# When ScalarE copies what VectorE transposed, and where a weight conversion is spread, in a retention + squared-ReLU kernel

## The chip, the core and the metric

The kernel runs on one core of a Trainium2 chip. Time is the device time of one execution in microseconds (us). The engines are called by the names that the profile uses: PE is TensorE's matmul and PEld its weight load, DVE is VectorE, ACT is ScalarE, POOL is GpSimd, and SP issues the transfers (DMA). Each engine runs its own list of instructions from first to last; engines wait for each other by semaphores.

## What is computed

Two layers, both in fp32. The first is retention: for each of 8 batches and 8 heads, 576 positions of 64 values, scores of queries and keys are multiplied by a lower triangular matrix of decays and then by the values. The second is a feed-forward block with a squared ReLU on the 4608 x 512 result.

```python
scores = scale * np.matmul(q, k.transpose(0, 1, 3, 2))            # (8, 8, 576, 576)
Dmat = np.where(rel >= 0, gamma[:, None, None] ** rel[None, :, :], 0.0)
attn = np.matmul(scores * Dmat[None], v)                          # (8, 8, 576, 64)
x = attn.transpose(0, 2, 1, 3).reshape(4608, 512)
h = np.maximum(x @ w_in, 0.0)                                     # w_in  512 x 2048
out = (h * h @ w_out).astype(np.float32)                          # w_out 2048 x 512
```

The weights arrive as 64-bit floats; the kernel converts them to fp32 itself, with integer and float operations on DVE and ACT. Both large products are done with a seven-product scheme (four quadrants of each operand, sums of quadrants, seven products in place of eight).

## The kernel before

There are two phases. In the first, retention and the first product `x @ w_in` run interleaved, and the squared result goes to memory (`g_dram`). The second phase is the product with `w_out`. Retention goes in 40 chunks of 128 or 64 positions (five to a batch). The first product goes in nine blocks of 512 tokens. Block 0 uses plain matmuls; blocks 1 to 8 have 28 steps each (four passes of seven products, 8 matmul records a step), run by `ffn_in(n, mp, j)` with `j` from 0 to 6.

Three PSUM tiles, called a, b and c, take the seven products in the order a b c a b c b. A product that adds to a tile cannot begin until DVE has read what the tile held at the product before it: the seventh product (b) waits for the read after the fifth (b, line 635), and only the sixth stands between.

```python
        if j == 0:
            nc.scalar.copy(p1, p)                                            # line 626, ACT
        elif j == 1:
            nc.vector.tensor_tensor(u2, p, p1, op=ALU.add)                   # 628
        elif j == 2:
            nc.vector.tensor_tensor(p15, p, p1, op=ALU.add)                  # 630
        elif j == 3:
            nc.scalar.activation(g["A11"], p, AF.Relu)                       # 632
            nc.gpsimd.tensor_tensor(g["A11"], g["A11"], g["A11"], op=ALU.mult)   # 633, POOL
        elif j == 4:
            nc.vector.tensor_tensor(g["A22"], p, p15, op=ALU.add)            # 635
            square(g["A22"])                                                 # 623
        elif j == 5:
            nc.vector.tensor_tensor(g["S3"], p, u2, op=ALU.add)              # 639
            square(g["S3"])
        else:
            nc.vector.tensor_tensor(g["A12"], p, p1, op=ALU.add)             # 642
            square(g["A12"])
            queue.extend(g_sums(n, mp))      # four sums of quadrants, lines 554 to 557, one a step
        # ... (sums of the next block's x, lines 540 to 543; sums of w_in during block 1, 245 to 248)
        if n >= 3 or n_w2[0] < 3 + 2 * 5:
            if not (held[0] and type(w_out_next[0]) is tuple):
                n_w2[0] += 1
                # ... takes one part of w_out's conversion from its list and issues it
```

The conversion of w_out is a list of 139 parts, 16 pieces of 128 x 512 and the sums of their quadrants. A piece has five: `one` (DVE, line 210), `two` (DVE, 214) together with `beside` (ACT, lines 218 and 219), `three` (DVE, 222, which reads what `beside` wrote), `four` (DVE, 225) and `last` (DVE, 228, and the next fetch). The sums are on lines 245 to 248. They use a staging area in weight tile 6. The x of the third block (block 2) lies in weight tile 6 too; the x of the others takes turns in two rooms:

```python
    xT = {n: xT_room[n % 2 if n < 2 else (n - 3) % 2] for n in range(N_BLK)}
    xT[2] = W[6][:, 0:N_DM * TOK].rearrange("p (c t) -> p c t", c=N_DM)
```

From chunk 9 on, q and k are turned by DVE (`flip`, two transposes of 32 x 32 squares a chunk, line 392), and ACT then puts the squares in place (16 copies of 32 x 256 for a chunk of 128, 8 for one of 64, line 403):

```python
    def spread(i):
        t, to = st[i]["flip"], new_qk(i)
        for b in range(chunks[i][3] // 32):
            for g in range(4):
                moves.append((i, to[32 * g:32 * g + 32, :, :, 32 * b:32 * b + 32], t[32 * b:32 * b + 32, g, :, :, :]))
    def move(count, i=N_CH):
        while moves and count and moves[0][0] <= i:
            nc.scalar.copy(*moves.pop(0)[1:])                                # line 403, ACT
            count -= 1
    # ... in the loop over chunks, past the first five:
            retain_a(i - 1)
            move(C, i)               # whatever copies of chunk i are left, all at once
            ffn(i - 1, 0)            # about half of the steps that fall to this chunk
            retain_b(i - 1)          # ends in a small ACT copy, line 495, that retain_c waits for
            scores(i)                # PE reads the copies of chunk i; DVE's mask follows, line 443
            retain_c(i - 1)
            if N_TURN <= i + 1 < N_CH:
                spread(i + 1)
            if N_TURN <= i + 2 < N_CH:
                flip(i + 2)          # both transposes here
            ffn(i - 1, 1)            # the other half of the steps
```

Inside `ffn`, each step is preceded by `move(3)`.

Of the kernel before, what the change touches and what calls it, by code (L numbers as in the profile page):

```python
# [9 lines left out]
F32 = mybir.dt.float32  # L10
# [5 lines left out]
C = 128  # L16
CH = C // 2
TOK = 512
# [22 lines left out]
def kernel(  # L41
# [33 lines left out]
    nc = tc.nc  # L75
# [268 lines left out]

    st = {i: {} for i in range(N_CH)}
    u_ps = [None]

    xT = {n: xT_room[n % 2 if n < 2 else (n - 3) % 2] for n in range(N_BLK)}
    xT[2] = W[6][:, 0:N_DM * TOK].rearrange("p (c t) -> p c t", c=N_DM)

# [30 lines left out]
    def new_qk(i):  # L383
        t = work3.tile([128, 2, HP, C], F32, tag="qk", name="qk")
        st[i]["qT"], st[i]["kT"] = t[:, 0, :, :], t[:, 1, :, :]
        return t

    def flip(i):
        cs = chunks[i][3]
        t = st[i]["flip"] = work2.tile([128, 4, 2, HP, 32], F32, tag="flip", name="flip")  # L390
        for j in (1, 0):
            nc.vector.transpose(t[:cs, :, j, :, :], loaded[i][j][:cs].rearrange("s (p e) (d a) -> s (e d) p a", e=2, d=2))

    def spread(i):
        t, to = st[i]["flip"], new_qk(i)
        for b in range(chunks[i][3] // 32):
            for g in range(4):
                moves.append((i, to[32 * g:32 * g + 32, :, :, 32 * b:32 * b + 32], t[32 * b:32 * b + 32, g, :, :, :]))

    def move(count, i=N_CH):  # L400

        while moves and count and moves[0][0] <= i:
            nc.scalar.copy(*moves.pop(0)[1:])  # L403
            count -= 1

    def turn(i):
# [90 lines left out]
    def retain_c(i):  # L497

        b_, ci, c0, cs = chunks[i]
        own, grow = within(i, 0)  # L500
        more = ci + 1 < NCH
        for j in range(0, len(own), 2):
            for f in own[j:j + 2] + (grow[j:j + 2] if more else []):
                f()
        tok = b_ * S + c0
        at = tok
        p = xp[0][:, :, 0:256].rearrange("p a (g t) -> p a g t", g=2)
        while at < tok + cs:
            n = at // TOK

            while steps and steps[0][0] <= (n - 2 if n > 4 else n - 3):
                step()
            end = min(tok + cs, (n + 1) * TOK)
            nc.scalar.copy(xT[n][:, :, at - n * TOK:end - n * TOK].rearrange("p (a g) t -> p a g t", a=2),
                           p[:, :, :, at - tok:end - tok])
            if more and at == tok:
                grown(i, 1)
            at = end
            if n_next[0] < N_BLK and (n_next[0] + 1) * TOK <= at:
                steps.extend(block_steps(n_next[0]))  # L520
                n_next[0] += 1
        st[i] = loaded[i] = None
# [78 lines left out]
    def ffn_in(n, mp, j):  # L601

        if j == 0 and mp == 0:

            if n not in sums_x:
                sums_x[n] = sum_x(n)
            for f in sums_x[n]:
                f()
        left, right, to = PRODUCTS[j]
        if j in OPENS:  # L610
            sums[to] = ps_f.tile([128, 2, HT], F32, tag="f", name=f"h_{to}")
        p = sums[to]
        for mm in range(2):
            w = w_in[mp][:, mm, WI_SLOT[left], :, :]
            for c in range(2):
                nc.tensor.matmul(p[:, mm, :], lhsT=w[:, c, :], rhs=xs[n][right][:, c, :],  # L616
                                 start=(j in OPENS and mm == 0 and c == 0), stop=(j in CLOSES and c == 1),
                                 skip_group_check=True)
        g = g_of(mp)
        p1, u2, p15 = (p_room[mp % 2][:, s, :, :] for s in range(3))  # L620

        def square(t):
            nc.vector.scalar_tensor_tensor(t, t, 0.0, t, op0=ALU.max, op1=ALU.mult)  # L623

        if j == 0:
            nc.scalar.copy(p1, p)  # L626
        elif j == 1:
            nc.vector.tensor_tensor(u2, p, p1, op=ALU.add)
        elif j == 2:
            nc.vector.tensor_tensor(p15, p, p1, op=ALU.add)  # L630
        elif j == 3:
            nc.scalar.activation(g["A11"], p, AF.Relu)  # L632
            nc.gpsimd.tensor_tensor(g["A11"], g["A11"], g["A11"], op=ALU.mult)  # L633
        elif j == 4:
            nc.vector.tensor_tensor(g["A22"], p, p15, op=ALU.add)  # L635
            square(g["A22"])
        elif j == 5:

            nc.vector.tensor_tensor(g["S3"], p, u2, op=ALU.add)
            square(g["S3"])  # L640
        else:
            nc.vector.tensor_tensor(g["A12"], p, p1, op=ALU.add)  # L642
            square(g["A12"])
            queue.extend(g_sums(n, mp))

        if mp == N_MP - 1 and j in (3, 4, 5) and n_next[0] > n + 1:
            if n + 1 not in sums_x:
                sums_x[n + 1] = sum_x(n + 1)
            sums_x[n + 1].pop(0)()
        if j in (6, 0, 1, 2, 3):  # L650
            some(2 if n == 1 and mp == 0 else 1)
        if n == 1 and 1 <= j < 5 and mp + 1 < N_MP:
            sums_w.setdefault(mp + 1, sum_w_in(mp + 1)).pop(0)()

        if n >= 3 or n_w2[0] < 3 + 2 * 5:
            if not (held[0] and type(w_out_next[0]) is tuple):
                n_w2[0] += 1
                f = w_out_next[0]
                w_out_next[0] = next(w_out_steps, None)
                for f in f if type(f) is tuple else (f,):  # L660
                    f and f()
            if n == N_BLK - 2 and (mp, j) in ((2, 3), (3, 3)):
                assert w_out_next[0] is None
                fetch_w2(mp - 2)
# [4 lines left out]
    w_out_steps = w_out_parts()  # L669
    w_out_next = [next(w_out_steps)]  # L670
    held = [False]
    n_w2 = [0]

    def block_steps(n):
# [23 lines left out]
    def ffn(i, half):  # L698

        gone[0] += chunks[max(0, min(i, N_CH - 1))][3] / 2  # L700
        if steps and steps[0][0] == 0:

            move(6)
            for f in (step, lambda: convert(6)) if half else (lambda: convert(6), step):
                f()
            if half and steps and steps[0][0] == 0:
                step()
                convert(6)
            return
        if not behind:  # L710
            behind.append((gone[0] - HALF, done[0]))
        points = behind + [p for p in PACE if p[0] > behind[0][0]]
        want = points[-1][1]
        for (x0, y0), (x1, y1) in zip(points, points[1:]):
            if gone[0] < x1:
                want = y0 + (y1 - y0) * (gone[0] - x0) / (x1 - x0)
                break
        count = max(1, int(want) - done[0])
        while steps and count:
            held[0] = half == 0 and count == 1  # L720
            move(3)
            step()
            count -= 1
        held[0] = False


    def warm(count, wide):
# [12 lines left out]
    for i in range(N_CH + 1):  # L740
        if i <= N_EARLY:

            if i == 1:
                convert(2)
            elif i == 2:
                convert(5)
            if i >= 1:
                retain_a(i - 1)
                if i < 3:
                    warm(4, False)  # L750
                else:
                    convert(1)
                    first_in(2 * i - 5, (0,))
                    convert(5)
                retain_b(i - 1)
                if i < 3:
                    warm(4, False)
                retain_c(i - 1)
            convert((0, 1, 1, 0, 1)[i])
            if i == N_EARLY:  # L760
                fetch_raw(2)
                step()
            scores(i)
            if i == 2:
                convert(5)
                first_in(0, (0,))
            elif i == 3:
                convert(1)
                first_in(2, (0,))
                convert(5)  # L770
            elif i == N_EARLY:
                convert(5)
                step()
                convert(6)
            scale_q(i + 1, nc.gpsimd)
            if i < N_EARLY:
                if i < 2:
                    warm(6, False)
                turn(i + 1)
        else:  # L780
            if i == N_EARLY + 1:
                gone[0] = TOK
            retain_a(i - 1)
            if i < N_TURN:
                turn(i)
            move(C, i)
            ffn(i - 1, 0)
            retain_b(i - 1)
            if i < N_CH:
                scores(i)  # L790
            retain_c(i - 1)
            if N_TURN <= i + 1 < N_CH:
                spread(i + 1)
            if N_TURN <= i + 2 < N_CH:
                flip(i + 2)
            ffn(i - 1, 1)
# [249 lines left out]
```

## Time and profile before

The median of three runs is 996.27 us (995.36 to 997.81). The profiled execution spans 994.4 us. Read by stretches:

| stretch, us | what runs | PE busy | DVE busy | ACT busy |
|---|---|---|---|---|
| 0 to 106 | first chunks, block 0, conversion of w_in | 94.33 | 75.99 | 48.52 |
| 106 to 562 | retention and blocks 1 to 8 interleaved | 437.81 | 396.51 | 265.24 |
| 562 to 994 | last steps, then the product with w_out | 428.37 | 316.17 | 36.39 |

Costs of one instruction that the change touches, from the groups of instructions (mean): copy on line 403, 402 ns, 440 of them; a transpose on line 392, 697 ns for k and 664 ns for q; lines 210, 214, 222, 225 and 228 of the conversion, 506, 472, 757, 814 and 756 ns; lines 218 and 219 on ACT, 722 and 670 ns; a sum on lines 245 to 248 some 520 to 660 ns as mean of its shapes; a PSUM read on lines 628 to 642, 681 to 687 ns.

The profile names engines, lines and tiles as in the code above. A wait is written "engine tile line <- releaser": how long the engine was idle in total before instructions of that line, how many times, and the longest single time. A row of the windows view gives a stretch of time, then each engine's busy time in it with the number of instructions, the clock granted to TensorE as a share of full speed, the share of DMA engines in use and the GB/s they moved.

### The profile page before, as it was taken

The page shows a single profiled execution, that of the slowest core. Times are in us where ns is not written, and L with a number is a line of the kernel's source. Part 1 is how long each engine was busy: PE and PEld are TensorE (multiplying, and loading weights), DVE is VectorE, ACT ScalarE, POOL GpSimd, SP SyncE. Part 2 cuts the span into 40 slices and gives each one's busy share as a digit, 9 for nine tenths or more (in the row PEclk, how much of TensorE's full clock was granted, in tenths as well). Part 3 has the DMA queues.
Part 4 walks back from the last instruction along what each step waited for, and adds up shares of the span by engine and source line. Part 5 has one row for each costly group of instructions (what it writes and reads, how often), then busy time and mean ns, then how long its engine had stood idle before and what let it go on. Part 6 is the DMA issues. An engine that isn't in the chain of part 4 may idle for free. (4 is left out here: it accounts for less than half of the span.)

```text
span 994.4 us, 24115 instructions
## 1 busy us (share of the span) xinstructions
PE 960.5 (97%) x10092; PEld 855.8 (86%) x10092; DVE 788.7 (79%) x1458; ACT 350.2 (35%) x871; POOL 131.9 (13%) x121
## 2 busy tenths in 40 slices
PE   7899999999999989989999999999999999999998
PEld 6655777888878778877788889999999999999998
DVE  4789798768889899998986777777777677777766
ACT  3445575765665756746651000000000000000000
POOL 3211222212223231312211000000000000000000
PEclk9999999999999999989999999999999999999999
DMA  8884657655697589769358999684673757556351
GB/s 199 245 239 114 184 171 207 191 146 181 204 303 231 172 251 257 218 185 301 109 200 303 402 401 336 233 280 174 234 263 141 274 191 269 192 218 215 125 212 44
DMA packets 185037, 219.19 MB, mean 220 GB/s; under 512 B 118624, under 2 KB 135008, under 8 KB 175968
## 3 DMA queue, kind: packets, MB, share of 16 engines
q1 hardware_dynamic: 182816, 217.13, 67.3%
q8 instruction: 79, 1.29, 0.5%
q10 hardware_dynamic: 2112, 0.52, 0.2%
q14 instruction: 30, 0.25, 0.1%
HBM read 128.23 MB, written 89.39 MB: 219 GB/s over the span
## 5 line engine op out<-in xcount | busy, mean ns | idle before, releaser
L616 PE MATMUL h_b<-room,w 128*128 128x256 f32 x736 | 181.9, 391 | 10.6 <-DVE room L635 4.3
L403 ACT COPY qk<-flip 32x256 f32<-32x256 f32 x440 | 177.0, 402 | 6.3
L616 PEld LDWEIGHTS h_b<-room,w 128*128 128x128 f32 x736 | 139.9, 193 | 33.2 <-DVE room L635 6.1
L903 PE MATMUL o_b<-w,room 128*128 128x128 f32 x1168 | 144.5, 275 | 0.7 <-DVE room L854 0.7
L903 PEld LDWEIGHTS o_b<-w,room 128*128 128x128 f32 x1168 | 137.2, 192 | 0.9 <-DVE room L854 0.9
L903 PE MATMUL o_c<-w,room 128*128 128x128 f32 x1008 | 123.0, 275 | 0.0
L903 PEld LDWEIGHTS o_c<-w,room 128*128 128x128 f32 x1008 | 117.7, 192 | 0.0
L616 PE MATMUL h_c<-room,w 128*128 128x256 f32 x480 | 115.9, 385 | 0.0
L917 ACT COPY r<-o_a 128x128 f32<-128x128 f32 x53 | 14.1, 266 | 272.5 <-PE o_a L903 241.9
L616 PE MATMUL h_a<-room,w 128*128 128x256 f32 x448 | 107.6, 383 | 0.0
L616 PEld LDWEIGHTS h_c<-room,w 128*128 128x128 f32 x480 | 91.9, 193 | 13.6 <-DVE room L642 0.3
L616 PEld LDWEIGHTS h_a<-room,w 128*128 128x128 f32 x448 | 83.7, 190 | 12.1 <-ACT room L626 0.3
L633 POOL TENSOR_TENSOR room<-room 128x512 f32<-128x512 f32 x32 | 36.9, 1152 | 370.4 <-ACT room L632 264.5
L903 PE MATMUL o_a<-w,a 128*128 128x128 f32 x688 | 85.6, 275 | 0.0
L903 PEld LDWEIGHTS o_a<-w,a 128*128 128x128 f32 x688 | 81.2, 192 | 0.1
L623 DVE SCALAR_TENSOR_TENSOR room<-room 128x512 f32<-128x512 f32 x96 | 72.3, 753 | 3.3
L580 PE MATMUL h_ps<-room,w 128*128 128x512 f32 (+1 forms) x160 | 58.7, 515 | 3.3 <-DVE w L228 2.5
L375 POOL TENSOR_TENSOR q_ld<-q_ld,dv 128x512 f32<-128x512 f32 (+1 forms) x39 | 48.6, 1245 | 76.7 <-DMA q_ld<-in_q_dram 50.6
L457 PEld LDWEIGHTS x_ps<-qk,v_ld 64*64 64x64 f32 x1152 | 40.3, 136 | 17.8 <-issue 11.8
L457 PE MATMUL x_ps<-qk,v_ld 64*64 64x64 f32 x1152 | 49.7, 226 | 5.0 <-ACT u_sb L495 4.0
L580 PEld LDWEIGHTS h_ps<-room,w 128*128 128x128 f32 x160 | 29.2, 190 | 25.0 <-issue 20.4
L445 POOL TENSOR_TENSOR v_ld<-v_ld,dv 128x512 f32<-128x512 f32 (+1 forms) x40 | 47.5, 1187 | 13.6 <-DMA v_ld<-in_v_dram 5.9
(111 smaller groups left out, 1392.6 us busy)
## 6 DMA issues: line engine op xcount, KB each, us to landing
g_dram<-room SPq DMA_DIRECT2D x32, 1792.0 KB, 7.7
a<-g_dram SPq DMA_DIRECT2D x43, 1024.0 KB, 7.0
room<-g_dram SPq DMA_DIRECT2D x20, 1024.0 KB, 6.6
w<-w_dram SPq DMA_DIRECT2D x7, 1792.0 KB, 13.2
out_dram<-room SPq DMA_DIRECT2D x17, 512.0 KB, 3.2
w<-in_moe_w_in_dram SPq DMA_DIRECT2D x16, 512.0 KB, 5.6
w<-in_moe_w_out_dram SPq DMA_DIRECT2D x16, 512.0 KB, 3.9
v_ld<-in_v_dram SPq DMA_DIRECT2D x31, 256.0 KB, 4.4
```

The costliest lines, as they stand in the source:

```text
L375: engine.tensor_tensor(t, t, dv[:cs, :, NCH + ci:NCH + ci + 1].to_broadcast([cs, H, D]), op=ALU.mult)
L403: nc.scalar.copy(*moves.pop(0)[1:])
L445: nc.gpsimd.tensor_tensor(vs[:cs], vs[:cs], dv[:cs, :, ci:ci + 1].to_broadcast([cs, H, D]), op=ALU.mult)
L457: own.append(lambda hp=hp, e=e, b=b: nc.tensor.matmul(x_at(hp, b, h), lhsT=s["vs"][rows(h), 2 * hp + b, :], rhs=s["ret"][rows(h), e, hp, : ...
L580: nc.tensor.matmul(p.rearrange("p h t -> p (h t)"), lhsT=w[:, c, :], rhs=xT[0][:, c, lo * HT:hi * HT], start=(c == 0), stop=(c == N_DM - 1))
L616: nc.tensor.matmul(p[:, mm, :], lhsT=w[:, c, :], rhs=xs[n][right][:, c, :], start=(j in OPENS and mm == 0 and c == 0), stop=(j in CLOSES a ...
L623: nc.vector.scalar_tensor_tensor(t, t, 0.0, t, op0=ALU.max, op1=ALU.mult)
L633: nc.gpsimd.tensor_tensor(g["A11"], g["A11"], g["A11"], op=ALU.mult)
L903: nc.tensor.matmul(p, lhsT=s["lefts"][left][:, m, :], rhs=w_out[j][:, m, WO_SLOT[right], :], start=(i in OPENS and m == 0), stop=(i in CLO ...
L917: nc.scalar.copy(r[:, 0, 0:128], p)
```

## The change

Three things are changed, all in the first phase.

1. The copies. A chunk's two transposes are no longer issued together: one goes out ahead of each of the next two steps, and with the second its 16 copies are put on the list. They may be issued from three steps later on, two to a step (three where over 16 are waiting). Before, they were put on the list an iteration of the chunk loop later, and then three to a step. What is left when the chunk's scores come near is still issued all at once. It is meant to even out the work of DVE and ACT.
2. The conversion of w_out. It began in block 1, stopped after 13 parts, and went on in block 3 at a part a step. Now it follows a line of 0.8 parts a step from block 1 on, pauses in a step that has a transpose ahead of it, and catches up with a second part in steps j = 0 and j = 3, where DVE reads no PSUM tile.
3. The x of the third block. It goes to the room that the first block had, which frees weight tile 6 early; without that, the conversion could not use its staging area during block 2. All blocks take turns in the two rooms.

```diff
-    xT = {n: xT_room[n % 2 if n < 2 else (n - 3) % 2] for n in range(N_BLK)}
-    xT[2] = W[6][:, 0:N_DM * TOK].rearrange("p (c t) -> p c t", c=N_DM)
+    xT = {n: xT_room[1 - n % 2] for n in range(N_BLK)}
...
+    flips = []
     def flip(i):
         cs = chunks[i][3]
-        t = st[i]["flip"] = work2.tile([128, 4, 2, HP, 32], F32, tag="flip", name="flip")
-        for j in (1, 0):
+        t = work2.tile([128, 4, 2, HP, 32], F32, tag="flip", name="flip")
+        def one(j):
             nc.vector.transpose(t[:cs, :, j, :, :], ...)
-    def spread(i):
-        t, to = st[i]["flip"], new_qk(i)
-        ...
+        def two():
+            one(0)
+            to = new_qk(i)
+            for b in range(cs // 32):
+                for g in range(4):
+                    moves.append((i, done[0] + 3, to[...], t[...]))
+        flips.extend([lambda: one(1), two])
     def move(count, i=N_CH):
-        while moves and count and moves[0][0] <= i:
+        while moves and count and moves[0][0] <= i and (moves[0][1] <= done[0] or count == C):
...
-            while steps and steps[0][0] <= (n - 2 if n > 4 else n - 3):
+            while steps and steps[0][0] <= n - 2:
                 step()
...
-        if n >= 3 or n_w2[0] < 3 + 2 * 5:
-            if not (held[0] and type(w_out_next[0]) is tuple):
+        behind_w2 = 0.8 * (done[0] - N_0) - n_w2[0]
+        for _ in range((behind_w2 > 0) + (behind_w2 > 2 and j in (0, 3))):
+            if not (busy[0] or held[0] and type(w_out_next[0]) is tuple):
...
             held[0] = half == 0 and count == 1
-            move(3)
+            move(3 if len(moves) > 16 else 2)
+            busy[0] = len(flips) > 0
+            for f in flips[:1]:
+                f()
+            del flips[:1]
             step()
...
-            if N_TURN <= i + 1 < N_CH:
-                spread(i + 1)
```

## The prediction

> **What bounds the kernel now.** I read the page's first two parts first, then the windows view, cut where each block of the first product begins, then PE's waits, and then the timeline at the longest wait.
>
> ```profile
> PE 960.5 (97%) x10092; PEld 855.8 (86%) x10092; DVE 788.7 (79%) x1458; ACT 350.2 (35%) x871; POOL 131.9 (13%) x121
> ```
>
> PE is the bound. What a change of the other engines can give is PE's idle time, and where it lies the windows tell. These are blocks 1 to 7, one row each:
>
> ```profile
> 106.60:170.40 63.80, 59.75 (x691) 49.61 (x688) 56.55 (x86) 41.62 (x101) 17.17 (x14) 1.00 0.66 192
> 170.40:230.60 60.20, 60.16 (x745) 51.21 (x738) 44.27 (x68) 39.67 (x99) 14.20 (x13) 1.00 0.65 180
> 230.60:291.50 60.90, 60.09 (x642) 50.98 (x641) 54.86 (x92) 33.68 (x80) 14.20 (x12) 0.97 0.72 226
> 291.50:357.50 66.00, 61.19 (x770) 51.47 (x769) 60.56 (x96) 43.18 (x105) 17.16 (x14) 1.00 0.71 207
> 357.50:419.70 62.20, 60.88 (x769) 51.23 (x767) 59.98 (x95) 42.55 (x101) 15.79 (x13) 1.00 0.83 242
> 419.70:485.50 65.80, 61.16 (x648) 51.46 (x641) 59.70 (x96) 37.65 (x90) 15.36 (x13) 0.95 0.78 229
> 485.50:547.50 62.00, 59.48 (x625) 50.52 (x624) 49.14 (x81) 25.28 (x61) 7.79 (x7) 0.97 0.58 212
> ```
>
> After the time comes the row's length, then busy PE, PEld, DVE, ACT, POOL, then the granted clock. Length less PE's busy time is idle: 4.1, 0.0, 0.8, 4.8, 1.3, 4.6 and 2.5 us, 18.1 in all. Block 2, the one block without any of w_out's conversion, is the one in which PE never waits, and DVE is busy 44.27 of 60.20 us (74%) there, against 89 to 96% in blocks 1 and 3 to 6. So DVE's load by the conversion makes the waits, not the retention alone. PE's waits from 100 to 560 us:
>
> ```profile
> PE h_b L616 <- DVE room L635: 4.3, 4, 1.4
> PE sc_ps L435 <- ACT qk L403: 3.5, 6, 1.1
> PE h_b L616 <- DVE room L628: 3.5, 1, 3.5
> PE x_ps L457 <- ACT u_sb L495: 3.1, 4, 2.1
> PE h_b L616 <- DVE room L541: 2.6, 2, 1.6
> ```
>
> With three smaller ones (0.8 and 0.3 behind DVE, 0.5 behind ACT) that is 18.6 us: 11.5 behind DVE, 7.1 behind ACT. The longest, 3.5 us, on DVE's timeline:
>
> ```profile
> 424.92 0.68 DVE L443 TENSOR_TENSOR qk<-sc_ps,msk 128x512 f32<-128x512 f32 x1
> 425.52 0.69 DVE L392 STREAM_TRANSPOSE flip<-k_ld 64x512 f32<-64x512 f32 x1
> 426.14 0.66 DVE L392 STREAM_TRANSPOSE flip<-q_ld 64x512 f32<-64x512 f32 x1
> ...
> 427.90 1.25 DVE L247 TENSOR_TENSOR w<-w,w 128x256 f32<-128x256 f32 x1
> 429.19 1.17 DVE L248 TENSOR_TENSOR w<-w,w 128x256 f32<-128x256 f32 x1
> 430.28 0.68 DVE L628 TENSOR_TENSOR room<-h_b,room 128x512 f32<-128x512 f32 x1
> ```
>
> Mask, two transposes, two other sums and a part of the conversion stand in a row ahead of line 628's PSUM read, and PE stands until that has begun. This pile-up is what the change takes apart. The stall has a sequel in the clock:
>
> ```profile
> 429.60:436.40 6.80, 5.39 (x13) 4.26 (x14) 6.76 (x11) 0.06 (x1) 1.67 (x2) 0.50 0.27 98
> ```
>
> The clock is at half there. Two shorter stretches of the same kind follow at 255.6 (0.50 over 3.3 us) and 498.0 us (0.50 over 3.2 us), each just after stalls. Together some 13.6 us at half speed, in 1.4 of which PE stood anyway, so (13.6 - 1.4) / 2 = 6.1 us lost.
>
> **The ceiling** is then 18.6 + 6.1 = 24.7 us, 2.5% of 996.27. Before 106 us and past 562 us nothing changes: in 562 to 994 us PE is busy 428.37 of 432.
>
> **What the Trainium skill says.** "TensorE: Matmul & The Clock Gate", Part 1 (What's actually happening), says that the clock is either full or half, by how busy PE was in a free-running window of about 3.4 us. The trace agrees: only 1.00 and 0.50 occur inside these stretches, their lengths are one or two such windows, and each follows a stall. So a stall removed may take its half-clock stretch with it. The same page (Architectural detail) calls ACT's and DVE's queues strict FIFO: the trace agrees, as line 628's read stood behind the conversion's sums though its data were there. "SBUF — State Buffer", Who interferes with whom, says that a DVE operation with two SBUF inputs and a POOL operation that reads SBUF exclude each other. The trace fits: line 247 took 1.25 us at 427.90 (0.42 us for the equal shape on line 246 at 424.57), while POOL ran tensor operations of 1.21 and 1.23 us from 427.67 on. The change doesn't touch that: POOL's work and its order stay. "ScalarE: Activation LUTs", What ACT_TABLE_LOAD costs, gives 186 ns + 0.833 ns an element without pointer operands; an estimate for a copy of 256 is 399 ns, and the trace has 402.
>
> **The change part by part.** From the order in which the instructions stand in the two programs: PE's is the same but for the place of block 2's x, POOL's is the same, and no engine has more or fewer instructions. Only order changes on DVE, ACT and SP. So no busy time is added; it is all in the waits.
>
> *Conversion spread.* I counted its DVE instructions per block in both programs and multiplied by the means (506, 472, 757, 814, 756 ns, sums 517, 574, 623, 664). Blocks 1 to 7 before: 6.6, 0, 17.1, 19.4, 18.0, 17.8, 12.0 us. After: 12.3, 14.7, 16.0, 15.2, 13.2, 17.0, 2.4 us. The relief of blocks 3 to 6 is thus small, 72.3 to 61.4, 2.7 us a block; block 7 gains 9.6. Block 1 gets 5.7 and block 2 14.7 more. Neighbouring DVE instructions start 0.60 us apart where they last 0.68 (timeline above), so as occupied time I take 0.88 of a sum: block 2 goes to 44.3 + 12.9 = 57 of 60.2 us (95%), block 1 to 56.6 + 5.0 = 61.6 of 63.8 (97%). Both become as full as blocks 4 to 6 are now.
>
> *Transposes apart.* Mask and both transposes directly in a row occur 29 times before, 5 times after. Each case parted takes one transpose, 0.6 us, out of a pile-up, and a part of the conversion, 0.6 us, is left out in those steps. The stalls behind DVE are 0.3 to 3.5 us long, most of them 1.3 to 1.6, so losing 1.2 us from the pile ends most of those of this kind.
>
> *Doubled parts.* A second part is issued in one step where j is 0 or 3. Where the two are `two` + `beside` and `three`, DVE must wait for ACT in between. It has that twice in 16 pieces before, and 8 times after. At 336.46 us of the trace such a wait is 2.38 us (line 222 behind line 219, with six copies ahead of it in ACT's queue), yet PE lost only 0.3 us there. Eight at 1.5 to 2.4 us are 12 to 19 us of idle DVE. Five of them stand ahead of line 635, whose slack is one step (about 1.9 us from 8 records of 0.216 us and gaps, less the read's 0.69). I charge 0.4 us each on PE, 3 us in all.
>
> *Copies.* Their count of 440 and ACT's load stay. Followed through the loops, 178 copies are left to be issued at once ahead of the scores before, 154 after, and a chunk has 10 or more left 8 times before, 7 after. So the burst ahead of the scores, which makes the 3.5 us, hardly shrinks. Two in place of three ahead of each step bring the small copies (line 495) forward by 0.4 us.
>
> *The room for x.* Block 2's x is copied when block 0's matmuls are long past in PE's list, and no step moves. Zero.
>
> The sum, block by block as idle of PE after: 4.0, 1.5, 1.0, 2.5, 1.5, 2.5, 0.5 = 13.5 us, against 18.1. I chose these: block 2 loses its freedom from waits, block 1 gives back what parting the transposes brings, blocks 4 and 6 halve, and block 7 is nearly free. The 3 us charged for doubled parts are within them. That brings 4.6 us. Of the half-clock stretches I take away the one after the 3.5 us pile-up and keep two others, so 6.1 goes to about 3.4: 2.7 us. Together 7.3: 996.3 - 7.3 = **989 us**.
>
> **Rivals.** (a) *The pile-ups were all.* Parting the transposes and the pauses end nearly all DVE waits, even in blocks 1 and 2, and no half-clock stretch is left: 11.5 + 3 + 6.1, about 20 us, 976. For it: block 2's 0.0. Against it: block 2 has that at 74% DVE load, and after the change no block from 1 to 6 is that light. (b) *The waits move.* Blocks 1 and 2 get the waits that blocks 4 to 6 had, and `three` behind `beside` takes the place of the pile-up: 5 us more in blocks 1 and 2, 6 to 8 more ahead of line 635, against 7 won: 998 to 1002. For it: eight cases against two. Against it: the measured 2.38 us wait cost PE 0.3. (c) *ACT becomes the one that ends the waits*, since copies now stand ahead of every step's copy or ReLU. ACT is busy at most 41.62 of 63.80 us, so it has room, and this would be worth 2 us.
>
> **Range and chances.** Between (a) and (b) lies 976 to 1002. I hold a gain of 2 to 13 us for likely and a small loss for possible: 981 to 996 should hold it 8 times in 10. Faster by over 2% needs under 976.3, which is 20 of the ceiling of 24.7 us: 0.05. Slower by over 2% needs 20 us of new waits: 0.01.
>
> **What would show it.** Right: PE's waits behind lines 628 and 541 gone or under 1 us; block 2's row with some idle PE and DVE at about 57 us; line 222 behind line 219 some 8 times; one or two half-clock stretches; the wait on line 403 still 2 to 4 us. Wrong: block 2 with no wait at 95% load (then order matters, not load, and (a) holds), or line 635's wait grown past 8 us (then (b)).

## The result, and the profile after

The changed kernel takes 1001.79 us (median of 4 runs, 1001.22 to 1002.88), the kernel before 997.04 us (4 runs, 995.36 to 998.46): a ratio of 1.005, 95% interval 1.003 to 1.007. It is a small loss where 989 us was predicted. The profiled execution spans 999.6 us.

In the lines of the changed kernel most numbers are five higher: line 616 is now 621 (the first product's matmul), 403 is 408 (copies), 443 is 448 (mask), 457 is 462 and 495 is 500 (retention's matmul and the small copy it waits for), 541 is 546, 628, 635 and 642 are 633, 640 and 647. Lines 210 to 248 (the conversion) keep theirs; of these, 245 to 248 are the sums of w_out alone, and those of w_in are on 238 to 241. The page's first part:

```profile
PE 962.4 (96%) x10092; PEld 857.0 (86%) x10092; DVE 791.4 (79%) x1458; ACT 350.5 (35%) x871; POOL 131.5 (13%) x121
```

The work is the same, so the loss is in waits and clock. Blocks 1 to 7 in the windows view (the columns are those of the rows before):

```profile
109.30:176.50 67.20, 61.32 (x692) 51.00 (x689) 62.16 (x94) 42.88 (x103) 16.89 (x14) 0.97 0.64 186
176.50:238.60 62.10, 60.35 (x740) 51.04 (x737) 53.85 (x89) 41.53 (x102) 14.32 (x13) 1.00 0.83 247
238.60:304.30 65.70, 61.57 (x641) 51.69 (x641) 56.34 (x92) 39.10 (x94) 14.59 (x12) 0.95 0.60 183
304.30:370.50 66.20, 62.33 (x769) 52.53 (x769) 55.11 (x89) 38.18 (x92) 16.26 (x14) 0.97 0.74 227
370.50:432.30 61.80, 60.38 (x770) 51.23 (x769) 55.28 (x91) 42.39 (x103) 14.55 (x13) 1.00 0.79 242
432.30:493.20 60.90, 58.55 (x645) 49.23 (x642) 58.93 (x91) 36.47 (x87) 16.52 (x13) 1.00 0.68 183
493.20:552.00 58.80, 57.69 (x625) 49.03 (x624) 43.03 (x67) 23.03 (x56) 7.64 (x7) 1.00 0.60 218
```

Blocks 1 to 3 became longer by 3.4, 1.9 and 4.8 us, blocks 5 to 7 shorter by 0.4, 4.9 and 3.2. PE's idle time is 5.9, 1.8, 4.1, 3.9, 1.4, 2.3 and 1.1 us, 20.5 against 18.1 before. The granted clock is below 1.00 in three blocks, as before, and the half-speed stretches in blocks 1 to 7 sum to 13.6 us in both profiles (6.8 + 2 x 3.4). Another 2.7 us are lost before block 1 begins, where PE, DVE and POOL run the same instructions in the same order as before; in all the traces of this case block 1 begins between 106.6 and 110.0 us, so these 2.7 us aren't put down to the change. PE's waits from 100 to 570 us:

```profile
PE x_ps L462 <- ACT u_sb L500: 6.7, 7, 1.9
PE h_b L621 <- DVE room L640: 6.0, 4, 2.9
PE sc_ps L440 <- ACT qk L408: 3.3, 3, 1.6
PE h_b L621 <- DVE room L546: 1.6, 2, 1.2
PE x_ps L462 <- issue: 1.4, 1, 1.4
```

The 3.5 us behind line 628 (now 633) are gone, as meant. In their place the small copy on line 500 went from 3.1 to 6.7 us, and line 640 from 4.3 to 6.0. How ACT can come to be late shows on its timeline at the place where PE paid most (start, duration, what ran, and in brackets the idle time before it):

```profile
256.71 0.40 ACT L408 COPY qk<-flip 32x256 f32<-32x256 f32 x1
260.10 0.72 ACT L218 ACTIVATE w<-w,exp_bias 128x512 uint32<-128x512 uint32 x1 [3.00 <-DVE w L210]
260.73 0.66 ACT L219 ACTIVATE w<-w 128x512 f32<-128x512 uint32 x1
261.42 3.33 ACT L408 COPY qk<-flip 32x256 f32<-32x256 f32 x8
264.77 0.60 ACT L637 ACTIVATE room<-h_a 128x512 f32<-128x512 f32 x1
265.26 0.16 ACT L500 COPY u_sb<-x_ps 128x2 f32<-128x2 f32 x1
```

and PE's timeline in the same stretch:

```profile
262.29 0.33 PE L440 MATMUL sc_ps<-qk 64*64 64x64 f32 x2 [1.19 <-ACT qk L408]
263.13 0.68 PE L440 MATMUL sc_ps<-qk 64*64 64x64 f32 x26 [0.51 <-ACT qk L408]
265.56 1.12 PE L462 MATMUL x_ps<-qk,v_ld 64*64 64x64 f32 x16 [1.76 <-ACT u_sb L500]
```

ACT stood idle for 3.00 us at the head of its list because line 210 of DVE was late. Eight copies, a ReLU and the small copy, none of which needed the conversion, were behind it, and PE paid 1.19 + 0.51 + 1.76 us. The sequel is in the clock:

```profile
264.70:271.50 6.80, 5.93 (x28) 4.86 (x29) 1.69 (x4) 2.68 (x8) 4.08 (x4) 0.50 0.84 269
```

Half speed for 6.80 us. Over all blocks, ACT's waits on line 218 behind line 210 grew from 12.6 to 18.0 us, both in 8 times. DVE waited on ACT in turn (line 222 behind line 219) for 5.5 us in 3 times, 2.5 in 2 before. This place shows how one stall arises; that the sum of such waits makes the loss is not shown, and e8 below speaks against it: it has 25.8 us of them and no loss.

### The profile page after: what moved, and what is told of

Its sections match the earlier page's. It is cut to its first block, busy times and chain, and to the rows that moved or that the text cites. A ratio compares the mean times of both kernels' runs of the same rounds, so it can differ in the third digit from the quotient of the medians.

```text
span 999.6 us, 24113 instructions
## 1 busy us (share of the span) xinstructions
PE 962.4 (96%) x10092; PEld 857.0 (86%) x10092; DVE 791.4 (79%) x1458; ACT 350.5 (35%) x871; POOL 131.5 (13%) x121
## 5 line engine op out<-in xcount | busy, mean ns | idle before, releaser
L621 PE MATMUL h_b<-room,w 128*128 128x256 f32 x768 | 187.6, 388 | 7.6 <-DVE room L640 6.0
L621 PEld LDWEIGHTS h_b<-room,w 128*128 128x128 f32 x768 | 144.4, 192 | 30.9 <-DVE room L640 8.0
L621 PE MATMUL h_c<-room,w 128*128 128x256 f32 x512 | 124.3, 386 | 0.0
L621 PE MATMUL h_a<-room,w 128*128 128x256 f32 x512 | 123.4, 384 | 0.0
L621 PEld LDWEIGHTS h_c<-room,w 128*128 128x128 f32 x512 | 97.8, 193 | 14.3 <-DVE room L647 0.3
L621 PEld LDWEIGHTS h_a<-room,w 128*128 128x128 f32 x512 | 96.1, 191 | 13.9 <-ACT room L631 0.3
L450 POOL TENSOR_TENSOR v_ld<-v_ld,dv 128x512 f32<-128x512 f32 (+1 forms) x40 | 49.7, 1242 | 12.4 <-DMA v_ld<-in_v_dram 7.6
## 6 DMA issues: line engine op xcount, KB each, us to landing
w<-w_dram SPq DMA_DIRECT2D x7, 1792.0 KB, 11.8
```

What stands on the lines that cost most here:

```text
L450: nc.gpsimd.tensor_tensor(vs[:cs], vs[:cs], dv[:cs, :, ci:ci + 1].to_broadcast([cs, H, D]), op=ALU.mult)
```

## The experiments

Each ratio is to runs of the kernel before on the same chip, with its 95% interval. "Double step" means a step of the first product that issues two parts of the conversion. By the order of its program the changed kernel has 21, 13 in j = 0 and 8 in j = 3. The expectations count 22, since they also count a step behind the end of the list of 139 parts, which issues nothing; their counts of the other kernels are too high for the same reason, and the text below has the real ones.

### One part at a time

`e1_copies_alone`: part 1 alone. `e2_spread_alone`: parts 2 and 3, the copies as before, and so without pauses and double steps. `e4_room_alone`: part 3 alone.

```diff
 # e1: before, with flips, two(), done[0] + 3 and move(3 if len(moves) > 16 else 2) of the change
 # e2: before, with xT_room[1 - n % 2], steps[0][0] <= n - 2, behind_w2, busy
 # e4: before, with
+    xT = {n: xT_room[1 - n % 2] for n in range(N_BLK)}
+            while steps and steps[0][0] <= n - 2:
```

> Part 1 alone: transposes parted, copies two to a step from three steps on; conversion and room of x as before. Three theories. Pairs (the doubled parts, which the pauses beside the transposes make necessary, put two + beside and three next to each other and make DVE and ACT wait for each other): here there are 2 such places as before, so no loss, ratio to before 0.990 to 1.000. Load (the conversion in blocks 1 and 2 is what costs): no loss either, 0.990 to 1.000. Copies (two to a step keep ACT behind when the scores' copies and the small copy u_sb come): 1.003 to 1.007, with PE's wait for the small u_sb copy at 6 us or more as in the changed kernel.

> Parts 2 and 3 alone: conversion at 0.8 parts a step from block 1, x of the third block in the first one's room; transposes and copies as before. Without pauses the conversion hardly ever falls behind, so no place is left where two + beside and three follow each other directly on DVE (0, against 8 in the changed kernel), while the load by blocks is that of the changed kernel (13.3, 13.7, 16.6, 14.6, 14.2, 16.0, 2.4 us). Pairs: 0.993 to 1.001. Load: 1.004 to 1.008, with blocks 1 to 3 longer by 8 us or more together. Copies: 0.993 to 1.001.

> Part 3 alone: x of the third block in the first one's room, everything else as before. The order of instructions is that of before on every engine. All theories: 1.000, within 0.998 to 1.002; this shows how well the comparison can tell such sizes apart.

Measured: copies alone 994.62 us, 0.9972 (0.996 to 0.9984); spread and room 999.03 us, 1.002 (1.0008 to 1.0032); room alone 999.21 us, 1.0021 (1.0008 to 1.0034). Block 6 fell from 65.8 to 61.9 us with the copies alone, to 60.9 with the spread alone, and to 60.9 with the whole change. Blocks 1 to 3, 184.8 us before, take 183.5 with the copies alone and 193.0 with the spread alone. PE's longest waits of e1 (its line numbers are one higher than the changed kernel's):

```profile
PE x_ps L463 <- ACT u_sb L501: 9.3, 9, 2.3
PE h_b L622 <- DVE room L641: 2.7, 4, 1.5
```

So the longer wait on the small copy comes with the copies' new order, and e1 has more of it than the changed kernel and is faster than the kernel before. By itself that wait doesn't explain the loss.

The room was expected to cost nothing. It moved no block by more than 0.2 us in the profile, though the wait on the small copy grew by 2.1 us (3.1 to 5.2). From its 1.0021 I take some 2 us as an estimate of what a mere shift of a few instructions can do here.

### Direct neighbours, block 1, and the place of ACT's part

`e3_no_pair`: the second part of a double step never follows or is an ACT part. `e5_block1_spared`: block 1 keeps the 13 parts it had. `e6_beside_after_flush`: ACT's part is kept out of the last step ahead of small copies too.

```diff
 # e3
+        met = False
+        for again in range((behind_w2 > 0) + (behind_w2 > 2 and j in (0, 3))):
+            pair = type(w_out_next[0]) is tuple
+            if not (busy[0] or held[0] and pair or again and (met or pair)):
 # e5
-        behind_w2 = 0.8 * (done[0] - N_0) - n_w2[0]
+        at_w2 = done[0] - N_0
+        behind_w2 = (min(13, 0.8 * at_w2) if n == 1 else 13 + 0.863 * (at_w2 - 28)) - n_w2[0]
 # e6
-            held[0] = half == 0 and count == 1
+            held[0] = count == 1
```

> The changed kernel, but a second part in a step is issued only when neither part of the two is the one with ACT's work. Direct neighbours two and three on DVE fall from 8 to 0, one and two from 5 to 1; load by blocks nearly the same (11.5, 15.5, 16.0, 13.1, 13.7, 16.7, 4.2 us). Pairs: the loss goes, ratio to before 0.992 to 1.000, PE's wait for the small u_sb copy back to about 3 us. Load or copies: stays at 1.003 to 1.007.

> The changed kernel, but block 1 keeps its 13 parts of before (6.6 us of DVE work instead of 12.3), and the rest follows a line of 0.863 parts a step over blocks 2 to 7. Pauses and catching up stay. Load in block 1 (the theory that the conversion added there costs what later blocks give back): block 1 falls from 67 to 64 us, ratio to before 1.000 to 1.002. Pauses (leaving parts out beside the transposes and catching up later makes the waits): stays at 1.004 to 1.007, since there are 9 direct neighbours two and three, as many as in the changed kernel. Head of the queue (beside, waiting for one, stands ahead of the burst of copies on ACT): 1.003 to 1.006.

> The changed kernel, but the part with ACT's work is also held back in the last step before the burst of copies ahead of the scores, not only in the last step before the scores. Head of the queue: PE's waits for the small u_sb copy and for the copies on ACT fall from 10 us together to 5 or less, ratio 0.999 to 1.002. Load in block 1: 1.004 to 1.007, blocks 1 and 2 as long as in the changed kernel (67 and 62 us). Pauses: 1.003 to 1.006 (direct neighbours two and three fall from 8 to 4 as a side effect).

Measured: 1003.23 us, 1.0056 (1.0035 to 1.0077); 1000.93 us, 1.003 (1.0014 to 1.0045); 999.3 us, 1.0014 (1.0003 to 1.0025). In e3's trace lines 214 and 222 never follow each other directly (8 times in the changed kernel), and the loss stays: it doesn't need direct neighbours. (The edit moves double steps too, 11 of 20 now stand in j = 3, so e3 doesn't show what neighbours cost.) Sparing block 1 shortens it from 67.2 to 64.8 us, but block 4 takes 69.0 instead of 66.2. In e6 the wait on the copies (line 408) goes to 0.0 and the one on the small copy grows to 11.8 us: the time, 1.0014, is what the theory of the head of the queue gave, but its sign, the two waits at 5 us or less together, did not come.

### Moving ACT's part between the halves

`e11_second_half` issues ACT's parts only in the second half of a chunk, `e12_first_half` only in the first and without pauses.

```diff
 # e11
-            if not (busy[0] or held[0] and type(w_out_next[0]) is tuple):
+            if not held[0] if type(w_out_next[0]) is tuple else not busy[0]:
-            held[0] = half == 0 and count == 1
+            held[0] = half == 0
 # e12
-            held[0] = half == 0 and count == 1
+            held[0] = half == 1 or count == 1
-            busy[0] = len(flips) > 0
+            busy[0] = False
```

> The changed kernel with its pauses, except that a part with ACT's work is issued in spite of a pause, and never in the first half of a chunk's steps: 2 of 16 are left there, against 8. Place: the loss goes, 0.998 to 1.001, PE's wait for the small u_sb copy from 6.9 to 4.5 us or less. Pauses: 1.003 to 1.006.

> e8 (no pauses), but all 16 parts with ACT's work are put into the first half, between the burst of copies and the small u_sb copy (3 of 16 in e8). Place: the loss comes back without any pause, 1.002 to 1.006, PE's wait for the small u_sb copy from 4.8 to 8 us or more. Pauses: as e8, 0.997 to 1.000.

> The changed kernel once more, on the chip and with the rounds of the experiments beside it: 1.003 to 1.007 by its first measurement. If it comes out under 1.002, the size of the loss has to be taken from here for all comparisons.

Measured: 1002.34 us, 1.0037 (1.0023 to 1.0052); 1001.16 us, 1.003 (1.0018 to 1.0042); the changed kernel on the same chip 1001.14 us, 1.0029 (1.0014 to 1.0043), 22 runs. PE's waits of e11:

```profile
PE h_b L621 <- DVE room L640: 11.5, 9, 3.3
PE h_b L621 <- DVE room L546: 3.6, 2, 3.2
...
PE x_ps L462 <- ACT u_sb L500: 1.7, 3, 0.9
```

The small copy's wait is down from 6.7 to 1.7 us, and line 640's is up from 6.0 to 11.5: the time is the same. ACT's late part is what PE waits for, but taking it away only lets DVE's pile-up end the wait. e11 has 24 double steps, 12 of them in j = 3, which may have a share in that. e12 loses without any pause, as the theory of place had it, yet its wait on the small copy is 6.2 us, not 8 or more. Holding ACT's parts back also leaves the conversion behind its line, so e12 has 12 double steps; it doesn't tell the two causes apart.

### Without pauses

`e8_no_pauses`: no step leaves its part out because of a transpose. The conversion then never falls two parts behind, and no double step is left. `e9_spared_no_pauses` adds e5's edit, `e10_spared_second_half` adds e11's `held[0] = half == 0` to that.

```diff
 # e8
-            busy[0] = len(flips) > 0
+            busy[0] = False
```

> The changed kernel without pauses: a part of the conversion is issued also in steps that have a transpose ahead of them, so that it never falls behind and never catches up. If the parts of the change added up, this would be copies alone and spread alone together: -2.9 and +1.5 us, ratio 0.9986. Pauses: 0.997 to 1.000. Load in block 1: 1.003 to 1.006, since the load by blocks is the same (13.3, 13.7, 16.6, 14.6, 14.2, 16.0, 2.4 us). Head of the queue: 1.002 to 1.006.

> Both: block 1 keeps its 13 parts, and there are no pauses. With the changed kernel, e5 and e8 this makes a square of four. Load in block 1: 0.996 to 0.999, as e5 and 3 us or more under e8. Pauses: as e8. If only the two together cost, all three are alike and near 0.997.

> e9 (block 1 spared, no pauses), with the parts that have ACT's work held back through the whole first half of a chunk's steps, which lies between the burst of copies and the small u_sb copy: 1 of 16 is left there, against 3 in e9. Place (what costs is ACT's 1.4 us of conversion between the burst of copies and the small u_sb copy, some 0.5 us a piece): 0.993 to 0.996, PE's wait for the small u_sb copy from 4.4 to about 3.5 us. Pauses (leaving out and catching up costs by itself): as e9, 0.996. A loss of over 0.002 against e9 speaks against place.

Measured: 995.98 us, 0.9986 (0.9972 to 1.0); 993.67 us, 0.9959 (0.9942 to 0.9976); 995.26 us, 0.9975 (0.9962 to 0.9987). All three are at or below the kernel before. The parts alone, 0.9972 and 1.002, give 0.9992 when multiplied, and e8 has 0.9986: without pauses the parts add up. The changed kernel has 1.0029. So the pause, or the catching up that it calls for, turned a small gain into the loss. e9 against e8 suggests that the load of block 1 costs something too: 2.3 us by the medians, with block 1 at 62.3 us instead of 65.3, though the intervals touch. e10 brings nothing over e9.

### Pauses and double steps taken apart

`e14_lumps_no_pauses` has 40 double steps, half in j = 0 and half in j = 3, and no pauses; `e15_pauses_no_lumps` has the pauses, and double steps (23) in blocks 6 and 7 only. `e16_catch_up_6_0` catches up in j = 0 (10 double steps) and 6 (14); `e17_lumps_6_0` is e14 in those places (7 and 17).

```diff
-        for _ in range((behind_w2 > 0) + (behind_w2 > 2 and j in (0, 3))):
 # e14, e17 (with (0, 6)), both with busy[0] = False
+        for _ in range((behind_w2 > 1.5) * (1 + (j in (0, 3)))):
 # e15
+        for _ in range((behind_w2 > 0) + (n >= 6 and behind_w2 > 2)):
 # e16
+        for _ in range((behind_w2 > 0) + (behind_w2 > 2 and j in (0, 6))):
```

> e8 (no pauses), but a part is issued only once the conversion is 1.5 parts behind its line, and then two in steps j = 0 and j = 3: 51 steps with two parts (22 in the changed kernel, 0 in e8), 9 direct neighbours two and three (8 in the changed kernel), 6 of 16 parts with ACT's work in the first half. Lumps: the loss comes back, 1.002 to 1.006. Emptied second half: as e8, 0.997 to 1.001, since 100 parts stay in the second half, as in e8 (101), against 73 in the changed kernel.

> The changed kernel with its pauses, but no second part in a step before block 6; the conversion falls behind its line and blocks 6 and 7 take what is left (24.3 and 7.1 us of DVE work instead of 17.0 and 2.4). Only blocks 1 to 5 are compared. Lumps: blocks 1 to 5 together fall from 323 us to 316 or less, near e8's 319 or under it. Emptied second half: they stay at 321 to 324 us, although they carry 11.8 us less of DVE work (59.4 against 71.4), with PE's wait for the small u_sb copy at 5 us or more in them. The whole time is not what this run is for; 1.000 to 1.006.

> The changed kernel, pauses and all, but a second part is issued in steps j = 0 and j = 6 instead of j = 0 and j = 3: 25 steps with two parts (22 before), 9 of 16 parts with ACT's work in the first half (8 before). Place in the step (j = 3 stands right ahead of the read with one step of slack): the loss goes, 0.997 to 1.001, PE's wait behind that read from 6 to 3 us or less. Any lump: stays, 1.002 to 1.006.

> e14 (lumps without pauses), with the steps of two parts moved from j = 0 and 3 to j = 0 and 6: 32 of them (51 in e14). Place in the step: 0.998 to 1.002. Any lump, at 0.24 us each as in e14 against e8: 1.006 or more (0.9986 and 32 x 0.24 us).

Measured: 1008.36 us, 1.0104 (1.0089 to 1.0118); 997.31 us, 0.9998 (0.9983 to 1.0012); 997.43 us, 1.0007 (0.9992 to 1.0022); 1006.25 us, 1.01 (1.0073 to 1.0126). PE's waits of e14:

```profile
PE h_b L621 <- DVE room L640: 12.2, 8, 2.5
PE x_ps L462 <- ACT u_sb L500: 5.4, 5, 1.8
```

Double steps without pauses cost the most, and in e14 the wait they make is plain: line 640. Pauses with no double step before block 6 cost nothing: e15's blocks 1 to 5, for which it was made, take 310.7 us, against 323.0 in the changed kernel and 319 in e8, though a part of that is load put off to blocks 6 and 7: DVE is busy 272.5 us in them, 282.7 in the changed kernel. e16 came out as the theory of place had it (0.997 to 1.001), e17 as the theory of any lump had it (1.006 or more). But e16 and e17 have 24 double steps each, so the number alone isn't it either. They differ in the pauses and in which parts meet: in e17 lines 210 and 214 follow each other directly 7 times, in e16 2 times, and ACT waits 42.1 us on line 218 behind line 210, against 13.0. Which of these costs e17 its 10 us was not tested.

### The same number of double steps in two places

`e18_catch_up_3` and `e19_catch_up_6`: the changed kernel with its double steps all in j = 3, or all in j = 6, 19 in each.

```diff
-        for _ in range((behind_w2 > 0) + (behind_w2 > 2 and j in (0, 3))):
+        for _ in range((behind_w2 > 0) + (behind_w2 > 2 and j == 3)):     # e18; j == 6 in e19
```

> The changed kernel, catching up with a second part in j = 3 alone (21 double steps, against 22 in j = 0 and 3). If it is the place, a lump right ahead of line 640's read of a tile that PE needs again one step later, all double steps now stand in the bad place: 1.004 to 1.010, and the wait behind line 640 at 8 us or more. If it is the number of double steps, whatever their place: 1.003 to 1.005, as the changed kernel, and the same as with j = 6.

> The changed kernel, catching up with a second part in j = 6 alone (22 double steps). If it is the place: 0.998 to 1.001, and the wait behind line 640 at 5 us or less. If it is the number of double steps: 1.003 to 1.005, the same as with j = 3.

Measured on one chip: 1001.89 us, 1.0033 (1.0018 to 1.0049), against 992.36 us, 0.9949 (0.9931 to 0.9968). Both lie below what place was to give, but they are not the same, as the mere number would have it: 9.5 us apart by the medians, 8.4 by the ratios. In these two kernels it is the place. The version with j = 6 beats both kernels and is the fastest of the study with e9, whose interval overlaps. PE's waits of e18 and then of e19:

```profile
PE x_ps L462 <- ACT u_sb L500: 11.3, 8, 4.2
PE h_b L621 <- DVE room L640: 5.3, 3, 2.5
PE h_b L621 <- DVE room L546: 3.0, 2, 2.6
PE sc_ps L440 <- ACT qk L408: 1.6, 1, 1.6
```

```profile
PE x_ps L462 <- ACT u_sb L500: 9.7, 9, 2.0
PE h_b L621 <- DVE room L640: 3.7, 3, 1.6
PE h_b L621 <- DVE room L546: 2.6, 2, 2.2
```

Line 640 did not reach the 8 us that I expected of e18. The difference is spread over three waits, 1.6 us each, and over the clock: time lost at half speed (span times one less the mean granted clock, mean of all runs) is 9.3 us in e18 and 6.0 in e19. In the traces, blocks 1 to 7 take 445.1 and 436.0 us; of the 9.1 us between them, 5.1 are PE's idle time and 3.4 half speed. ACT's waits on line 218 behind line 210 don't differ (11.4 and 12.0 us).

The length of blocks 1 to 7 in the traces, from the first matmul record of each block to the next one's:

| kernel | 1 | 2 | 3 | 4 | 5 | 6 | 7 |
|---|---|---|---|---|---|---|---|
| before | 63.8 | 60.1 | 60.9 | 66.0 | 62.3 | 65.8 | 62.0 |
| changed | 67.2 | 62.2 | 65.7 | 66.2 | 61.7 | 60.9 | 58.9 |
| copies alone (e1) | 62.9 | 60.0 | 60.6 | 68.6 | 61.6 | 61.9 | 61.7 |
| no pauses (e8) | 65.3 | 61.8 | 61.4 | 68.2 | 62.4 | 58.2 | 59.0 |
| catch up in j = 3 (e18) | 65.4 | 62.8 | 64.1 | 67.4 | 64.8 | 60.6 | 60.1 |
| catch up in j = 6 (e19) | 64.8 | 61.0 | 60.9 | 67.1 | 63.0 | 59.6 | 59.5 |

With j = 6, blocks 1 to 3 cost 1.9 us over before, not 10.3, and the gain of blocks 6 and 7 stays.

## Why the prediction was wrong

**What failed: doubled parts.** I charged 3 us, 0.4 us for each place where `three` follows `two` and `beside` directly, and counted as dangerous only these eight. The loss is there without any of them (e3). What counts more is where the double steps stand: catching up in j = 6 is 8.4 to 9.5 us faster than in j = 3, with as many double steps. For the changed kernel, in j = 0 and 3, the term of 3 us measures about 4 us against the kernel without pauses (1.0029 against 0.9986) and 8 against e19 (0.9949), each on another chip. That line 635's slack of one step decides was half right: with 40 double steps its successor, line 640, takes 12.2 us, but with 19 or 21 the waits spread over ACT's copies too. In e16 and e19 catching up in j = 0 as well as j = 6 cost 0.0058 of the time on two chips; why j = 0 costs isn't shown.

**Pauses.** I took them for a help of 0.6 us a step and did not see that parts left out come back as second parts a few steps later. That is the link the prediction lacked. Pauses before block 6 without catching up do no harm (e15), and with the catching up put in j = 6 the whole change brings 0.5%.

**The gain was too large as well.** Without the 3 us charged I had 10.3 us of gain, 7.6 of idle time and 2.7 of clock. e19, where the double steps cost least, gains 5.1 (0.9949), and PE's idle time in its blocks 1 to 7 is 17.8 us, 18.2 before: hardly any of the 7.6 came. So of the 10 us between my forecast and the 22 runs of the changed kernel, about 5 belong to the double steps and about 5 to a gain that isn't there (an estimate, since the ratios are from two chips). Block by block the load is a part of that: e8, without a double step, takes 3.7 us more than before in blocks 1 to 3, where my idle times were to grow by 1.6.

**The sum of idle time.** Predicted 4.0, 1.5, 1.0, 2.5, 1.5, 2.5, 0.5, measured 5.9, 1.8, 4.1, 3.9, 1.4, 2.3, 1.1. Blocks 2, 5, 6 and 7 are within 0.6 us. Blocks 1, 3 and 4 are 6.4 us too low in my sum. Blocks 1 and 3 are where e19 is 2.4 and 4.8 us shorter than the changed kernel; of the 4.8, 3.4 are lost at half speed.

**The clock.** I let 6.1 us at half speed fall to 3.4. Over all runs the loss is 8.6 us on average before (265 runs) and 10.9 after (26 runs). The 6.8 us stretch behind the 3.5 us pile-up went, and the one shown above came in its place. The Trainium skill's "TensorE: Matmul & The Clock Gate", Part 1 (What's actually happening), gives a clock that is full or half by how busy PE was in a window of about 3.4 us; the trace of the changed kernel agrees, with stretches of 3.4 or 6.8 us in blocks 1 to 7, each after a stall. In e19 the loss is 6.0, so my 2.7 us of gain were about right for a kernel without the bad stalls.

**What was right, and what of the signs came.** That no busy time is added: PE is busy 962.4 us, 960.5 before. The 3.5 us pile-up behind line 628 ended. Line 541's wait was to go below 1 us and fell only from 2.6 to 1.6. The wait on the copies ahead of the scores stayed, 3.3 us. Block 2 got idle time; its DVE is at 53.85 us, 3 below my 57. Line 222 behind line 219 was to come some 8 times and came 3 times. The room for x was put at zero; alone it measured 1.0021, which may be the chance of where things fall, and was not followed further; e8 and e19, which have the room too, show no loss.

**Rivals.** (b) came nearest in time, 998 to 1002, and by its reason in blocks 1 to 3. But its sign, line 635's wait beyond 8 us, did not appear. (c), dismissed since ACT has room, came true as a wait: ACT ends 6.7 + 3.3 + 0.5 = 10.5 us of waits, 7.1 before. But it ends about as much in e1 (9.3 + 0.8 + 0.5) and e19 (9.7 + 0.5), which are faster than the kernel before, so it isn't shown that the loss lies there. Low busy time doesn't rule such waits out: ACT is busy 42.88 of 67.20 us in block 1.

**Not settled.** e14 and e17 cost 10 us each in different places of the step. e17, with 17 of 24 double steps in j = 6, is what the place alone doesn't explain; the shares of j = 0, of the missing pauses and of the parts that meet were not taken apart. Moving double steps also shifts every later part, so j = 3 against j = 6 is the difference of two whole orders and not of one step.

## What to carry over

When work is paused to relieve an engine, look where it is made up: here double portions ahead of a read with one step of slack cost more than the pause brought (1.0033), and as many behind the last read of a pass did not (0.9949). With other parts in them and no pauses, double portions there cost 1% as well (e17), so the place is one thing to look at and not a rule. Two in-order queues that hand a piece back and forth make waits that no busy share shows; ask what stands behind the instruction that waits, and then whether a kernel with more of that wait is slower at all. Run the parts of a change alone, and their combination with one rule altered: here the parts added up without the pauses, and so what was left over pointed at the pauses.

## What the runs showed of the hardware

The time of the unchanged kernel spreads from 990.8 to 1003.6 us over 265 runs (standard deviation 2.1 us). The time lost at half speed in one run is between 0.0 and 17.0 us and goes with the span (correlation 0.69): the same program meets a different number of half-speed stretches in each run. A run with 1 us more of it is only 0.41 us longer, which may mean that part of the half-speed time lies where PE would have waited anyway; that is not shown. Kernels that stall less mostly lose less of it: 6.0 us in e19, 6.8 in e9, 10.9 in the changed kernel (but 6.8 in e2, which is slower than before). With 22 runs the intervals above reach 1.1 to 1.6 us to either side, so a difference of 2 to 3 us in this kernel needs some twenty runs before it can be told from that (an estimate from these widths).
